# Sparse attention and a mixture of depths on one core: last queries' units in pairs, the gate row through DRAM, the mixture over 27 steps

## The chip, the cores and the metric

The kernel runs on one core of a Trainium2 chip. The metric is the time of one execution in microseconds (us). The core's engines are TensorE (PE, its weight loads PEld), VectorE (DVE), ScalarE (ACT), GpSimd (POOL) and SyncE (SP, which here only issues DMAs).

## The reference

Attention in which each query keeps the 32 largest scores of its row, then a layer in which each batch's 128 tokens with the largest gate go through a small network. B is 8 batches, H 8 heads, S 576 tokens, D 64; the bridged width is 512, the network's hidden width F 1024.

```python
scores = (1 / sqrt(D)) * q @ k.T                    # per batch and head
kth = np.partition(scores, -32, axis=-1)[..., -32:-31]
scores = np.where(scores >= kth, scores, -1e9)
attn = softmax(scores)                              # with + 1e-09 in the denominator
x = (attn @ v) -> (B, S, H * D)
# mixture: per batch b
s = x[b] @ w_gate
top = the 128 tokens with the largest s
ye = relu(x[b, top] @ w1) @ w2
out[b, top] = x[b, top] + sigmoid(s[top])[:, None] * ye     # other rows: x
```

## The kernel before

All data is float32. The 576 queries of a batch are four tiles of 128 (`t` 0 to 3, token 4p + t on partition p) and a last one of 64 (`t == J`). A unit is one query tile and one pair of heads; a unit of `t < J` holds two tiles of [128, 576] scores, one for each head. In a unit of last queries the two heads' 64 rows are stacked into one tile. A batch has 16 units of two tiles and 4 of one tile, 20 in all; eight batches make 160.

The main loop is a software pipeline written out by hand. Step `n` works on six units at once; every engine takes its instructions in the order in which the loop issues them:

- unit `n + 1`: `multiply` (PE, products of q and k into the PSUM tile `ps`) and `keep` (ACT, `sc`);
- unit `n`: `find_bound` (DVE: maxima of eighths `cand`, then three rounds of `best`), a bound below which no score can be among the 32;
- unit `n - 1`: `cut` and `part` (ACT, `sides`), then on POOL `y = sc * sides` and `fill`;
- unit `n - 2`: `find_kth` (DVE, `next8`), the 32nd score;
- unit `n - 3`: `mask` (`less`): the first tile on ACT, a second one on POOL;
- unit `n - 4`: `turn` and `turn_last` (PE: each 128-wide block of scores is turned and out-of-reach scores are pushed down by a second matmul with `less`; eight blocks into `ptr`, and the last 64 keys of both tiles as a ninth into a corner of `ps`), exponentials (ACT, `pT` and `last`), `values` (PE, into `av`) and `keep_values` (ACT, `xs`).

`ps` has one buffer, so the products of a step wait until ACT has read the turned last block. When a query tile's heads are done, two steps follow it: DVE inverts the sums (`sums`, `rden`), and POOL writes `x` (`normalise`) and DVE the gate product (`gates`, `prod`). After `t == J` SP stores `x` to `out`.

The mixture of batch `b - 1` is a generator that the loop advances by one piece in each step of batch `b` from `mix_at` on: the gate row is turned on PE and copied by ACT so that it stands on every partition (`gate_row`, two pieces); DVE counts for each token how many gates are larger (`junk`, `ranks`) and marks its place (`pick`), in three pieces; PE and DVE make the row numbers (`place_ps`, `row_i`); POOL gathers the rows (`xe`, an indirect DMA); PE turns them and DVE makes their gate (`xe_ps`, `g`); three pieces of the first layer (`h_ps`, 12, 12 and 8 matmuls), four of the second (`y_ps`, two each); ACT scales (`gy`), POOL adds the rows to `out` by an indirect DMA (the scatter). The next batch's q and k rows are fetched by SP and turned by PE at the steps of `load_at` (`rows`, `tr`). In the trace each float32 matmul of the program stands as two.

PSUM rooms named `misc` (one buffer) serve row transposes, gate transposes and all mixture products in turn.

Of the kernel before, what the change touches and what calls it, by code (L numbers as in the profile page):

```python
# [45 lines left out]
def kernel(  # L46
# [36 lines left out]
    modpool = ctx.enter_context(tc.tile_pool(name="mod", bufs=1))  # L83
    PS = bass.MemoryType.PSUM
# [37 lines left out]
    NS = B * NHP * (2 * J + 1)  # L122
# [20 lines left out]
    for i in range(2):  # L143
        vt = const.tile([P, H, J, DE], FP32, name=f"v{i}")
        nc.gpsimd.memset(vt, 1.0)
        vlast = const.tile([R, H, DE], FP32, name=f"vlast{i}")
        nc.gpsimd.memset(vlast, 1.0)
# [4 lines left out]
        vbufs.append((vt, vlast, vpair))  # L152
# [96 lines left out]
    def load_v(vb, vs):  # L249
        vt, vlast, vpair = vs  # L250
        v_rows = vb[:, JP:S, :].rearrange("h p d -> p h d")
        sp.dma_start(out=vlast[:, :, 0:D], in_=v_rows)
# [10 lines left out]
    def heads_of(t):  # L263

        return [[(0, 0), (1, R)]] if t == J else [[(0, 0)], [(1, 0)]]
# [4 lines left out]
    def multiply(t, hp, kT, qT, ps):  # L274
# [16 lines left out]
    def keep(n, ps):  # L291

        sc = scpool.tile([P, 2, S], FP32, name="sc")
        for i in range(n):
# [6 lines left out]
    def find_bound(n, sc):  # L301
# [7 lines left out]
        for i in range(n):  # L309
            for u in range(8):  # L310
                dve.max(cand[:, i, 8 * u : 8 * u + 8], sc[:, i, u * w : (u + 1) * w])
        for r in range(3):
            for i in range(n):
                dve.max(best[r][:, i, :], cand[:, i, :])
            if r < 2:
                for i in range(n):
# [5 lines left out]
    def cut(n, best, at):  # L322

        act.copy(
            out=seen[:, 0, at : at + n],
            in_=best.rearrange("p i e -> p (i e)").bitcast(BF16)[:, 15 : 16 * n : 16],
        )
# [16 lines left out]
    def fill(n, y, at):  # L344

        pool.tensor_tensor(
            y[:, 0:n, S : S + 8],
            steps[:, 0:n, :],
            seen[:, 2, at : at + n].unsqueeze(2).to_broadcast([P, n, 8]),
# [3 lines left out]
    def find_kth(n, y):  # L353

        next8 = stats.tile([P, 2, 8], FP32, name="next8")
        for i in range(n):
# [3 lines left out]
    def mask(n, sc, next8):  # L360

        less = wkpool.tile([P, 2, S], BF16, name="less")
        for i in range(n):
# [33 lines left out]
    def turn_last(n, z, ps, less=None):  # L397
# [4 lines left out]
        tr = ps[0 : n * R, 1, 1, 512 - P : 512]  # L402
        last = [
            a and a.rearrange("p i s -> p (i s)")[:, JP : JP + n * R] for a in (z, less)
# [4 lines left out]
    def values(t, hp, i, pT, last, av, vs):  # L409

        vt, vlast, vpair = vs
        n = R if t == J else P
        for hh, r in heads_of(t)[i]:
            o = av[0:n, hh * DE : (hh + 1) * DE]
            for c in range(J):
                pe.matmul(
                    o,
                    pT[:, i, c, r : r + n],
                    vt[:, 2 * hp + hh, c, :],
                    start=(c == 0 and i == 0),  # L420
                    stop=(c == J - 1 and t < J),
                    skip_group_check=(i == 1),
                )
            if t == J:
                pe.matmul(
                    o,
                    last[0:R, r : r + n],
                    vlast[:, 2 * hp + hh, :],
                    start=False,
                    stop=True,  # L430
                )
# [3 lines left out]
        if i == 1:  # L435
# [9 lines left out]
    def keep_values(t, hp, av, xs):  # L445
        n = R if t == J else P
        act.copy(
            out=xs[0:n, 2 * hp : 2 * hp + 2, :].rearrange("p h e -> p (h e)"),
            in_=av[0:n, 0 : 2 * DE],
        )  # L450
# [53 lines left out]
    def mixture(row0, gate, rank, exact=False):  # L504
# [7 lines left out]
        tr = ps_misc.tile([P, 512], FP32, name="tr", tag="misc")  # L512
        for t in range(J):
            pe.transpose(
                tr[:, t * P : (t + 1) * P],
                gate[:, t : t + 1].to_broadcast([P, P]),
                ident,
            )
        late.append(lambda tr=tr: act.copy(out=gate_row[:, 0:JP], in_=tr))

        yield
        tr = ps_misc.tile([P, 512], FP32, name="tr", tag="misc")
        pe.transpose(
            tr[:, 0:R], gate[0:R, J:NT].to_broadcast([R, P]), ident[0:R, 0:R]
        )
        late.append(lambda tr=tr: act.copy(out=gate_row[:, JP:S], in_=tr[:, 0:R]))
# [3 lines left out]
        for t in range(NT):  # L530
            if t % 2 == 0:
                yield
# [57 lines left out]
        yield  # L590
# [92 lines left out]
    units = [(b, t, hp) for b in range(B) for t in range(NT) for hp in range(NHP)]  # L683
    per_batch = NT * NHP


    load_at = (0, 1, 10, 11, 12, 13, 16, 17, 18)
# [8 lines left out]
    mix_at = 14  # L696
    first_tile, tiles = [], 0
    for b, t, hp in units:
        first_tile.append(tiles)
        tiles += len(heads_of(t))  # L700
# [268 lines left out]
```

## Time and profile before

| | us |
|---|---|
| median of 3 runs | 1003.89 (1003.25 to 1007.76) |
| profiled execution, own time | 1007.97 |
| its span (first to last instruction) | 1006.2 |
| PE busy | 948.5 (94%) |
| DVE busy | 866.1 (86%) |
| ACT busy | 804.9 (80%) |
| POOL busy | 709.5 (71%) |

The profiled execution lies 1.8 us over its span and 0.4% over the median. A busy share is a mean over the whole span; batches and single steps are read with windows. A step is taken from the start of one unit's last-block turn on PE to that of the next.

### The profile page before, as it was taken

To read this page: it belongs to the slowest core of one execution; us is meant where nothing else is said; L and a number is where in the kernel's file an instruction comes from. 1 tells how busy PE (TensorE), PEld (TensorE's weight loads), DVE (VectorE), ACT (ScalarE), POOL (GpSimd) and SP (SyncE) were. 2 spreads that over 40 slices of the span, in tenths; PEclk is the share of its full clock that TensorE was granted. 3 is DMA by queue.
4 is the path that set the end of the run, shared out by engine and by line. 5 is a ranking of instruction groups with operands and counts; after the bars stand their busy time and mean duration, and the time that the engine had idled before them with its cause. 6 is when DMAs were issued, how large, how long until landed. Compare 5 with 4: busy or idle time off the path is not lost.

```text
span 1006.2 us, 24785 instructions
## 1 busy us (share of the span) xinstructions
PE 948.5 (94%) x7922; PEld 760.4 (76%) x7922; DVE 866.1 (86%) x4966; ACT 804.9 (80%) x1945; POOL 709.5 (71%) x818
## 2 busy tenths in 40 slices
PE   5799999999999999999999999999999999999856
PEld 3588777786878878887878878788778878777734
DVE  4899899999989998899988998899988999899130
ACT  3799899998779887898889897898889987797300
POOL 3688768984778767895778857886768957797110
PEclk9999999999999999999999999999999999999778
DMA  5942012112203112111212122111122010000110
GB/s 107 260 95 56 2 53 59 39 37 75 60 1 65 33 65 58 33 38 43 76 32 54 32 75 59 21 44 44 53 59 38 17 54 7 1 12 2 53 26 14
DMA packets 123833, 49.12 MB, mean 49 GB/s; under 512 B 118960, under 2 KB 118960, under 8 KB 122672
## 3 DMA queue, kind: packets, MB, share of 16 engines
q1 hardware_dynamic: 120320, 42.88, 16.8%
q0 software_dynamic: 1792, 4.20, 2.3%
q8 instruction: 65, 1.06, 0.4%
q10 hardware_dynamic: 1584, 0.39, 0.2%
q14 instruction: 72, 0.59, 0.2%
HBM read 35.91 MB, written 11.53 MB: 47 GB/s over the span
## 4 chain that ended last, share of the span: by engine, by line
PE 59%; ACT 15%; DVE 14%; POOL 8%; issue 2%; DMA 1%; SPq 0%; ACTq 0%; POOLq 0%
PE av L42 19%; PE ps L42 13%; PE ptr L42 13%; PE h_ps L42 6%; DVE cand L42 6%; PE y_ps L42 5%; ACT sides L42 5%; POOL y L42 4%; ACT sc L42 4%; DVE next L42 3%; POOL less L42 3%; PE tr L42 2%; ACT pT L42 2%; DVE best L42 2%; ACT less L42 1%
## 5 line engine op out<-in xcount | busy, mean ns | idle before, releaser
L42 POOL TENSOR_TENSOR y<-sc,sides 128x576 f32<-128x576 f32 x288 | 369.9, 1314 | 176.1 <-ACT sides L42 170.4
L42 DVE MAX8 cand<-sc 128x8 f32<-128x72 f32 x2304 | 323.8, 217 | 36.5 <-ACT sc L42 36.4
L42 PEld LDWEIGHTS av<-v,pT 128*128 128x128 f32 (+1 forms) x2560 | 274.8, 182 | 68.1 <-issue 26.1
L42 PE MATMUL av<-v,pT 128*128 128x65 f32 (+1 forms) x2560 | 301.6, 269 | 2.8 <-ACT pT L42 2.8
L42 DVE MAX8 next<-y 128x8 f32<-128x584 f32 x288 | 206.6, 754 | 35.7 <-POOL y L42 35.5
L42 POOL TENSOR_SCALAR less<-sc,next 128x576 bf16<-128x576 f32 x128 | 224.1, 1751 | 4.8 <-DVE next L42 4.3
L42 ACT ACTIVATE sides<-sc,seen 128x576 bf16<-128x576 f32 x288 | 221.3, 769 | 7.4
L42 PE MATMUL ptr<-ident,sc 128*128 128x128 f32 x1152 | 217.8, 281 | 0.0
L42 PE MATMUL ps<-kT,qT 64*128 64x288 f32 (+1 forms) x1280 | 203.2, 437 | 10.7 <-ACT last L42 5.8
L42 ACT ACTIVATE pT<-ptr 128x512 f32<-128x512 f32 x288 | 168.9, 596 | 50.7 <-PE ptr L42 42.7
L42 PE MATMUL ptr<-out_of_reach,less 128*128 128x128 bf16 x1152 | 206.4, 220 | 0.0
L42 ACT COPY sc<-ps 128x576 f32<-128x576 f32 x288 | 171.3, 646 | 10.6 <-PE ps L42 10.6
L42 PEld LDWEIGHTS ptr<-ident,sc 128*128 128x128 f32 x1152 | 162.7, 141 | 15.8
L42 DVE MAX8 best<-cand 128x8 f32<-128x64 f32 x864 | 154.5, 216 | 3.3
L42 PEld LDWEIGHTS <-less 128*128 128x128 bf16 (+1 forms) x1312 | 137.3, 105 | 23.2 <-POOL less L42 11.2
L42 PEld LDWEIGHTS ps<-kT,qT 64*128 64x128 f32 (+1 forms) x1280 | 106.3, 180 | 59.1 <-issue 20.8
L42 ACT ACTIVATE less<-sc,next 128x576 bf16<-128x576 f32 x160 | 124.4, 777 | 6.8 <-DVE next L42 6.5
L42 DVE MATCH_REPLACE8 cand<-best,cand 128x64 f32<-128x64 f32 x576 | 116.5, 209 | 0.0
L42 ACT ACTIVATE last<-ps 128x128 f32<-128x128 f32 (+1 forms) x160 | 43.8, 274 | 57.7 <-PE ps L42 56.9
L42 PE MATMUL h_ps<-xeT,w 128*128 128x128 f32 x512 | 66.5, 289 | 3.1 <-ACT hT L42 1.7
L42 PEld LDWEIGHTS h_ps<-xeT,w 128*128 128x128 f32 x512 | 63.1, 203 | 5.1 <-ACT hT L42 2.4
L42 POOL TENSOR_TENSOR x<-xs,rden 128x512 f32<-128x512 f32 (+1 forms) x40 | 41.7, 1042 | 33.6 <-DVE rden L42 33.6
(83 smaller groups left out, 919.2 us busy)
## 6 DMA issues: line engine op xcount, KB each, us to landing
rows<-in_k_dram SPq DMA_DIRECT2D x64, 128.0 KB, 2.9
v<-in_v_dram SPq DMA_DIRECT2D x64, 128.0 KB, 3.0
out_dram<-x SPq DMA_DIRECT2D x8, 1024.0 KB, 4.8
rows<-in_q_dram SPq DMA_DIRECT2D x62, 128.0 KB, 2.7
w<-in_moe_w_dram SPq DMA_DIRECT2D x2, 2048.0 KB, 13.4
last<-in_k_dram SPq DMA_DIRECT2D x8, 128.0 KB, 3.7
vlast<-in_v_dram SPq DMA_DIRECT2D x8, 128.0 KB, 3.0
vpair<-in_v_dram SPq DMA_DIRECT2D x16, 64.0 KB, 2.8
```

What stands on the lines that cost most here:

```text
L42: return lambda *a, **kw: self._tc.keep_in_program_order(fn(*a, **kw))
```

## The change

1. A unit of last queries now holds four heads in two tiles: in each tile two heads are stacked, heads 4g and 4g + 2 in the first, 4g + 1 and 4g + 3 in the second. Their products use four quarters of PE's array (rows by the head's half of the partitions, columns by its place in the stack), their values two column halves in turn. The last keys' values of such units come from the zero-padded `vpair` as for all others; `vlast` and its DMA are gone. Each batch has 18 units of two tiles, so every step is of one size, and the helper functions lose the argument for the number of tiles.
2. The gate row goes through DRAM: two DMAs write the gates in token order, a third reads them back onto all partitions. The last batch's mixture (`over`) still turns it on PE.
3. The mixture has 17 pieces, each rank of its own, at the steps of a table `mix_at` that reaches over two batches, so that two mixtures overlap; the first piece runs in step 5 of the next batch. After the last unit the loop advances the last but one mixture by two pieces a step. `load_at` is spread differently as well.

Here the step of a batch is n modulo 18; units of last queries have their values in steps 2 and 3 and their products in steps 15 and 16.

```diff
-        vlast = const.tile([R, H, DE], FP32, name=f"vlast{i}")
...
-        sp.dma_start(out=vlast[:, :, 0:D], in_=v_rows)
...
-    def heads_of(t):
-        return [[(0, 0), (1, R)]] if t == J else [[(0, 0)], [(1, 0)]]
+    def groups(t):
+        return NHP // 2 if t == J else NHP
+    def heads_of(t, g):
+        if t == J:
+            return [[(4 * g + i, 0), (4 * g + 2 + i, R)] for i in range(2)]
+        return [[(2 * g + i, 0)] for i in range(2)]
...
-    def multiply(t, hp, kT, qT, ps):
+    def multiply(t, g, kT, qT, ps):
         n = R if t == J else P
         for u in range(2):
-            for i, heads in enumerate(heads_of(t)):
+            for i, heads in enumerate(heads_of(t, g)):
                 at = u * HALF + (0 if i else R)
-                for hh, r in heads:
-                    d = slice(hh * D, (hh + 1) * D)
+                d = slice(i * D, (i + 1) * D)
+                for h, r in heads:
                     pe.matmul(
                         ps[r : r + n, i, u, 0:HALF],
-                        qT[d, hp, t * P : t * P + n],
-                        kT[d, hp, at : at + HALF],
+                        qT[d, h // 2, t * P : t * P + n],
+                        kT[d, h // 2, at : at + HALF],
                     )
...
+        for i, heads in enumerate(heads_of(t, g)):
             for c in range(J):
+                for h, r in heads:
+                    pe.matmul(
+                        av[r : r + n, i * DE : (i + 1) * DE],
+                        pT[:, i, c, r : r + n],
+                        vt[:, h, c, :],
...
+        for h, r in heads_of(t, g)[0]:
             pe.matmul(
-                av[:, 0 : 2 * DE],
-                last,
-                vpair[:, hp, :, :].rearrange("p h e -> p (h e)"),
+                av[r : r + n, 0 : 2 * DE],
+                last[:, r : r + n],
+                vpair[:, h // 2, :, :].rearrange("p h e -> p (h e)"),
...
+            row_dram = drampool.tile([1, S], FP32, name="row_dram")
+            sp.dma_start(
+                out=row_dram[0, 0:JP].rearrange("(p j) -> p j", j=J), in_=gate[:, 0:J]
+            )
+            sp.dma_start(
+                out=row_dram[0, JP:S].rearrange("(p j) -> p j", j=1),
+                in_=gate[0:R, J:NT],
+            )
+            sp.dma_start(out=gate_row, in_=row_dram.to_broadcast([P, S]))
...
         for t in range(NT):
-            if t % 2 == 0:
-                yield
+            yield
...
-    load_at = (0, 1, 10, 11, 12, 13, 16, 17, 18)
+    load_at = (2, 4, 6, 8, 14, 15, 16, 17, 18)
...
-    mix_at = 14
+    mix_at = (5, 7, 9, 10, 11, 12, 13, 14, 19, 21, 23, 25, 27, 28, 29, 30, 31)
...
+        for b in mix_steps.get(n, ()):
+            next(mixtures[b], None)
+        if n >= N:
+            for _ in range(2):
+                next(mixtures[B - 2], None)
+                flush()
```

PE, values of a one-tile unit of last queries in the last step of a batch's four (the names are the PSUM and SBUF tiles; `x4` counts the program's matmuls), before:

```order
L42 MATMUL ps<-kT,qT 128x288 x4
L42 MATMUL av<-v_124,pT 64x65 x4
L42 MATMUL av<-vlast_126,last 64x65
L42 MATMUL av<-v_124,pT 64x65 x4
L42 MATMUL av<-vlast_126,last 64x65
L42 MATMUL h_ps<-xeT,w_141 128x128 x12
```

and the second of a batch's two merged units after the change:

```order
L42 MATMUL ps<-kT,qT 128x288 x4
L42 MATMUL av<-v_132,pT 64x65 x16
L42 MATMUL av<-vpair_134,last 64x130 x2
L42 MATMUL h_ps<-xeT,w_139 128x128 x12
L42 MATMUL ps<-ident,sc 128x128
```

Four such groups of ten matmuls a batch have become two of eighteen, and the separate `vlast` matmuls are gone.

SP's DMAs from the store of a batch's `x` to the next batch's rows and values, before:

```order
L42 DMA out_dram<-x 128x2048
L42 DMA out_dram<-x 64x512
L42 DMA vlast_126<-in_v_dram 64x8x64
L42 DMA vpair_128<-in_v_dram 64x4x64 x2
L42 DMA v_124<-in_v_dram 128x4x64 x8
L42 DMA rows<-in_k_dram 128x4x64 x2
```

after:

```order
L42 DMA out_dram<-x 128x2048
L42 DMA out_dram<-x 64x512
L42 DMA row_dram<-gate 128x4
L42 DMA row_dram<-gate 64x1
L42 DMA gate_row<-row_dram 128x576
L42 DMA rows<-in_k_dram 128x4x64 x2
L42 DMA vpair_128<-in_v_dram 64x4x64 x2
```

Three DMAs now stand between the store of `x` and the next batch's rows and values.

## Rows read from the trace of the kernel before

**Rows 1.** The page, part 1: busy us, share, instructions.

```profile
PE 948.5 (94%) x7922; PEld 760.4 (76%) x7922; DVE 866.1 (86%) x4966; ACT 804.9 (80%) x1945; POOL 709.5 (71%) x818
```

**Rows 2.** Windows over batches 0, 1, 4 and 6 (columns in the first line).

```profile
core 0: us, PE busy (x) PEld busy (x) DVE busy (x) ACT busy (x) POOL busy (x), PEclk, DMA share, GB/s
37.32:143.89 106.57, 103.05 (x908) 83.78 (x909) 99.32 (x594) 97.58 (x240) 83.82 (x98) 1.00 0.32 82
...
143.89:255.69 111.80, 106.54 (x937) 86.77 (x936) 110.66 (x617) 99.78 (x244) 88.65 (x102) 0.98 0.19 47
...
488.06:604.25 116.19, 115.04 (x992) 93.27 (x991) 107.02 (x619) 100.26 (x243) 87.89 (x100) 1.00 0.20 48
...
720.45:835.04 114.59, 113.91 (x981) 92.26 (x979) 105.45 (x616) 98.54 (x237) 87.11 (x99) 1.00 0.15 37
```

**Rows 3.** Windows over single steps: row transposes, gate transposes, one-tile unit, plain step.

```profile
534.21:539.56 5.35, 5.35 (x51) 4.62 (x50) 3.73 (x24) 5.32 (x14) 4.17 (x5) 1.00 0.59 98
550.25:556.01 5.76, 5.52 (x50) 4.57 (x49) 5.76 (x36) 5.46 (x14) 5.08 (x7) 1.00 0.40 91
...
587.07:591.70 4.63, 4.63 (x44) 3.49 (x43) 4.60 (x34) 3.64 (x10) 2.56 (x4) 1.00 0.01 4
...
875.84:880.75 4.91, 4.91 (x45) 4.17 (x44) 3.04 (x16) 4.02 (x9) 4.76 (x6) 1.00 0.00 2
```

**Rows 4.** Timeline of PE, plain step from 875.84: start, us, instructions.

```profile
877.47 1.24 PE L42 MATMUL ps<-kT,qT 64*128 64x288 f32 x8
878.64 2.00 PE L42 MATMUL av<-v,pT 128*128 128x65 f32 x16
...
880.75 0.27 PE L42 MATMUL ps<-ident,sc 128*128 128x128 f32 x1
```

**Rows 5.** Timeline of PE, products and values of a one-tile step.

```profile
477.56 1.24 PE L42 MATMUL ps<-kT,qT 64*128 64x288 f32 x8 [0.77 <-ACT last L42]
478.73 0.68 PE L42 MATMUL av<-v,pT 128*64 128x65 f32 x8
479.34 0.33 PE L42 MATMUL av<-vlast,last 64*64 64x65 f32 x2
...
480.46 0.66 PE L42 MATMUL xe_ps<-ident,xe 128*128 128x128 f32 x4
```

**Rows 6.** Timeline of PE, products of a one-tile unit and what follows.

```profile
568.15 1.19 PE L42 MATMUL ps<-kT,qT 64*64 64x288 f32 x8
569.26 2.00 PE L42 MATMUL av<-v,pT 128*128 128x65 f32 x16
```

**Rows 7.** Timeline of PE and DVE behind the last values.

```profile
957.43 7.13 PE L42 MATMUL y_ps<-w,hT 128*128 128x512 f32 x16
...
960.06 0.07 DVE L42 DVE_READ_ACCUMULATOR2_ANT gate<- 64x1 f32 x1
...
965.35 0.65 PE L42 MATMUL tr<-ident,gate 128*128 128x128 f32 x4 [0.78 <-ACT gy L42]
```

**Rows 8.** DMA issues: KB each, median us from issue to landing.

```profile
rows<-in_k_dram SPq DMA_DIRECT2D x64, 128.0 KB, 2.9
...
out_dram<-x SPq DMA_DIRECT2D x8, 128.0 KB, 2.3
...
out_dram<-gy,row_i POOLq DMA_INDIRECT x8, 4.9
```

**Rows 9.** Chain of waits in batch 1: bounds and 32nd scores on DVE.

```profile
159.07 2.16 DVE cand L42 x16
...
162.79 1.33 DVE next L42 x2
...
212.56 1.09 DVE cand L42 x8
...
215.07 1.34 DVE next L42 x2
```

**Rows 10.** The page, part 5: busy us, mean ns of one.

```profile
L42 PEld LDWEIGHTS av<-v,pT 128*128 128x128 f32 (+1 forms) x2560 | 274.8, 182 | 68.1 <-issue 26.1
```

**Rows 11.** Groups of DVE in batch 4: busy us, mean ns of one.

```profile
L42 DVE CUSTOM_DVE_ANT_0 prod<-xe,wg 128x512 f32<-128x512 f32 x1 | 1.5, 1519 | 0.0
```

More of the change, by code (lines that the diff above doesn't have):

```diff
@@ L308, in find_bound @@
         best = [stats.tile([P, 2, 8], FP32, name=f"best{r}") for r in range(3)]
-        for i in range(n):
+        for i in range(2):
             for u in range(8):
@@ L502, in break_ties, with mixture @@
         )
-    def mixture(row0, gate, rank, exact=False):
+    def mixture(row0, gate, rank, exact=False, over=False):
         gate_row = modpool.tile([P, S], FP32, name="gate_row")
[L512 to L517, printed above, removed]
-            )
-        late.append(lambda tr=tr: act.copy(out=gate_row[:, 0:JP], in_=tr))
-        yield
[L522 to L526, printed above, removed]
+        if exact or over:
+            for t0, t1, at in ((0, J, 0), (J, NT, JP)):
+                tr = ps_misc.tile([P, 512], FP32, name="tr", tag="misc")
+                n = R if t0 else P
+                for t in range(t0, t1):
+                    pe.transpose(
+                        tr[:, (t - t0) * P : (t - t0) * P + n],
+                        gate[0:n, t : t + 1].to_broadcast([n, P]),
+                        ident[0:n, 0:n],
+                    )
+                w = (t1 - t0) * n
+                act.copy(out=gate_row[:, at : at + w], in_=tr[:, 0:w])
+        else:
+            row_dram = drampool.tile([1, S], FP32, name="row_dram")
+            sp.dma_start(
+                out=row_dram[0, 0:JP].rearrange("(p j) -> p j", j=J), in_=gate[:, 0:J]
+            )
+            sp.dma_start(
+                out=row_dram[0, JP:S].rearrange("(p j) -> p j", j=1),
+                in_=gate[0:R, J:NT],
+            )
+            sp.dma_start(out=gate_row, in_=row_dram.to_broadcast([P, S]))
         pick = modpool.tile([P, NT, CAP], BF16, name="pick")
         for t in range(NT):
-            if t % 2 == 0:
-                yield
+            yield
             n = R if t == J else P
@@ L694 @@
     v_at = 6
-    mix_at = 14
[L697 to L700, printed above, removed]
+    mix_at = (5, 7, 9, 10, 11, 12, 13, 14, 19, 21, 23, 25, 27, 28, 29, 30, 31)
+    mix_steps = {}
+    for b in range(B - 1):
+        for i in mix_at:
+            n = (b + 1) * per_batch + i
+            if n >= N:
+                break
+            mix_steps.setdefault(n, []).append(b)
+    mixtures = {}
     qkv = {0: room_for_qkv(0)}
@@ L709, with is_unit @@
     scs, bests, ys, next8s, masks = {}, {}, {}, {}, {}
-    def tiles_of(n):
-        return len(heads_of(units[n][1])) if 0 <= n < len(units) else 0
-    for n in range(-1, len(units) + 6):
+    def is_unit(n):
+        return 0 <= n < N
+    for n in range(-1, N + 6):
         if 0 <= n + 1 < NHP:
@@ L804 @@
                 store(out[b], of_batch[b][0])
-        b, i = divmod(n, per_batch)
-        if 0 < b < B and i == mix_at:
-            mixing = mixture(float((b - 1) * S), of_batch[b - 1][1], ranks[:, b - 1, :])
-        next(mixing, None)
-        if n >= len(units):
-            flush()
-            next(mixing, None)
+                mixtures[b] = mixture(
+                    float(b * S), of_batch[b][1], ranks[:, b, :], over=(b == B - 1)
+                )
+        for b in mix_steps.get(n, ()):
+            next(mixtures[b], None)
+        if n >= N:
+            for _ in range(2):
+                next(mixtures[B - 2], None)
+                flush()
         if n in load_steps:
@@ L822 @@
     flush()
-    for _ in mixing:
-        flush()
-    for _ in mixture(float((B - 1) * S), of_batch[B - 1][1], ranks[:, B - 1, :]):
-        flush()
+    for b in (B - 2, B - 1):
+        for _ in mixtures[b]:
+            flush()
     sure = stats.tile([P, 1], FP32, name="sure")
@@ L860, with general_weights @@
     )
-    def general_weights(n, sc):
+    def general_weights(sc):
         p = wkpool.tile([P, 2, S], FP32, name="p", tag="y")
-        for i in range(n):
+        for i in range(2):
             cur, tops = sc[:, i, :], []
@@ L911, in general @@
                 last = ptpool.tile([P, P], FP32, name="last")
-                for i in range(w):
+                for i in range(2):
                     nc.scalar.copy(
@@ L916, in general @@
                     )
-                nc.scalar.copy(out=last[0 : w * R, :], in_=turn_last(w, p, ps))
-                for i in range(w):
-                    values(t, hp, i, pT, last, av, vs)
-                keep_values(t, hp, av, xs)
+                nc.scalar.copy(out=last, in_=turn_last(p, ps))
+                values(t, g, pT, last, av, vs)
+                keep_values(t, g, av, xs)
             rows = R if t == J else P
```

163 lines of the change are left out of this document (73 added, 90 removed).

## The prediction

> **What bounds the kernel now.** I read the page's busy shares first, then windows over whole batches, then windows over single steps, then TensorE's (PE's) timeline inside a step, and the chain of waits where PE is not the bound. PE is busy for 94% of the span, VectorE (DVE) for 86% [rows 1]. By batches [rows 2] the reader is to see two regimes. In the steady ones (488.06 to 604.25; three more read the same) PE is busy for 115.04 of 116.19 us, DVE for 107.02. In the batch from 143.89, where half of a mixture of experts is missing on PE, DVE is busy for 110.66 of 111.80. So PE bounds batches 2 to 6, and DVE stands 8 us behind it.
>
> By steps [rows 3]: a plain step takes 4.91 us, all of it PE's, with DVE at 3.04. A step with four row transposes takes 5.35 (so they cost 0.44), one with the four gate transposes has 5.52 of PE, and a step that turns one tile of last queries takes 4.63 with four row transposes, 4.19 without. Inside the plain step [rows 4]: the nine turned blocks end at 877.47 (1.63 us), the scores' products at 878.64 (1.17), the values at 880.75 (2.11). Inside a one-tile step [rows 5] the products start 0.77 late, since ScalarE (ACT) must first read the last block out of the same PSUM tile; then 1.17 for products and 1.73 for values. That leaves 4.19 - 1.17 - 1.73 = 1.29 for turning.
>
> **The change, part by part.** All sums are for one steady batch, against 116.19.
>
> *Merged units.* A batch now has four one-tile value steps at 4.19, four steps whose products are those of last queries, and twelve plain ones. Such products run on two quarters of the array, in 1.11 [rows 6], so these steps take 4.91 - 1.17 + 1.11 = 4.85. Sum: 12 x 4.91 + 4 x 4.85 + 4 x 4.19 = 95.1. The rest of PE's 115.04, 19.9, is row transposes, mixture and gate transposes.
>
> After the change there are 14 plain steps (68.7), two with merged products of time M and two with merged values of time V. They take 3.74 + M and 1.63 + 1.17 + V = 2.80 + V.
>
> M: twice as many matmuls as the 1.11 holds, now on four quarters. If all four run side by side M stays 1.11; if only two do, it is 2.2. The row nearest is that same one: eight matmuls of 288 columns in 1.11 us. Sixteen y matmuls of 512 columns take 7.13 [rows 7], 0.87 ns a column, so eight of 288 one after another would need 2.0: quarters that share neither rows nor columns do run in pairs now. What no row shows is two quarters that share rows. I take 1.11. By the Trainium skill (TensorEngine Tiling (Array Packing), Key Properties) tiles work independently and load and multiply in parallel, which would give this same 1.11 and the low end for V; no row here has two such tiles.
>
> V: 32 matmuls of 64 weight columns that move 65 columns, and four that move 130, in alternating column halves. One after another: eight now take 0.61 (478.73 to 479.34) [rows 5], 0.076 each, so 2.43, plus four times 130 columns at 0.87 ns, 0.45: 2.9. Side by side in twos: 1.45. Loading weights may bind either way, and the mode no longer changes for the last block, which it did four times in 1.73; I take 2.0, just below the middle.
>
> So PE's steps come to 68.7 + 2 x 4.85 + 2 x 4.8 = 88.0; ends 86.9 (1.11 and 1.45) and 92.0 (2.2 and 2.9). The gain is 7.1 of PE, between 3.1 and 8.2.
>
> *Gate row through DRAM.* It removes five transposes: four cost 5.52 - 4.91 = 0.61 [rows 3, 4], so 0.8 with the fifth, and one read of each from PSUM by ACT. It adds three DMAs on SP, behind the store of x: two small writes that wait for the last gate product on DVE, and a read that waits for both. The nearest rows land in 2.3 and 2.9 us [rows 8], so 5 to 8 us with the issues (the read moves 295 KB). The first rank comes two steps later, over 10 us. Hidden at no cost; with that cover gone DVE would stall for the excess. Behind the waiting SP stand the next batch's rows and values. Rows are fetched three or more steps ahead of their transposes, so nothing waits for them.
>
> *Spread mixture.* PE's mixture work is only moved, and PE was continuous in the steps that held it, so the move itself saves little there. It puts ranks of one batch (DVE) beside y products of the one before (PE, four steps), which keeps DVE's extra work in PE's longest steps. The scatter is now one step ahead of the next gather, which must wait for its landing, 4.9 us [rows 8]; a step of 5.2 covers it on GpSimd (POOL).
>
> *DVE and POOL.* Bounds for two tiles cost DVE 3.72 (159.07 to 162.79), for a lone tile 2.51 (212.56 to 215.07) [rows 9]. Four lone tiles less save 4 x (2.51 - 1.86) = 2.6: DVE's busy time goes to 104.4. A plain step's own work on DVE is 5.05 (159.07 to 162.79 and 1.33 more). POOL gets two masks more and ACT two fewer; POOL has 28 us to spare a batch [rows 2].
>
> *Sum.* PE: 115.04 - 7.1 - 0.8 = 107.1, ends 106.0 and 111.1. Of the 1.15 that PE idles now, 0.77 stands ahead of a one-tile step's products and goes, as a full set of blocks lies there. But DVE, at 104.4, is now only 2.7 behind, and in step 1 of a batch it needs 5.05 + 1.5 for the gathered rows' gate [rows 11] + 0.2 where PE needs 4.91 + 0.5. It may trail by a step without stopping PE, so I add 1.4: 108.5 a batch, 7.7 less.
>
> - Batches 2 to 5: 4 x 7.7 = 31; batch 6, now 114.59, 6.
> - Batch 0 (106.57 now, 103.05 of PE, 99.32 of DVE): PE falls by 7, DVE stays near 97, and the first step's waits remain: 100.5, 6 less.
> - Batch 1: on DVE already, so the 2.6, two steps' hand-overs, and a little of the rank work that now lies later: 107, 5 less.
> - Batch 7 and the end: 8 for its units. Then the end: last values were done at 957.43, but 7.13 of y stood between them and the last batch's gate transposes at 965.35, although the gate itself was ready at 960.1 [rows 7]. With two steps of mixture 6 in each draining step, about half of y is left there: 4 less. 12 together.
>
> 31 + 6 + 6 + 5 + 12 = 60: the span goes from 1006.2 to 946, the profiled execution from 1007.97 to 948. The three runs have a median of 1003.89, 0.4% under the profiled one, so **944 us**.
>
> **Rivals.**
> 1. *Quarters in the same rows take turns* (M 2.2, V 2.9): the merging then does not do what it is for, and only saved blocks and mode changes remain. PE 111.1, batch 112; 4 x 4.2 + 2.6 + 4 + 5 + 9 = 37: 966. For it: no row shows such an overlap. Against it: loads and products of values, all in the same rows, already overlap, since 18 take 2.11, 0.117 each [rows 4], while one load alone lasts 0.18 [rows 10]. By the Trainium skill (TensorE: Matmul & The Clock Gate, The mechanism) a weight load overlaps matmuls in flight only where the row group differs, and here it never does: that is this rival's time. The rows of this kernel disagree with it in its strict form.
> 2. *DVE becomes the bound.* If no step lends time to the next, each takes the longer of PE and DVE. By the new order DVE exceeds PE by 1.3 in step 1, by 0.8 in step 13 (a gate product and the row numbers), by 0.5 in step 17 and by 0.5 in four others together: 3.1 over 107.1. Batch 110.2: 4 x 6.0 + 4.4 + 6 + 5 + 10 = 49: about 954. For it: batch 1 now. Against it: PE had no gap in the steps in which DVE trailed.
> 3. *Slower: each change of quarter drains the array.* A one-tile step's 20 value matmuls would stream in 20 x 65 x 0.87 ns = 1.1 but take 1.73: up to 0.15 for each of four changes of mode. If a change of half cost 0.1 as well, 2 x (35 + 15) changes make 10 us a batch on top of rival 1's 112: 122, and 1003.9 + 6 x 5.8 - 4 = 1035. It is slower from 0.04 a change on. Against it: plain products alternate between the array's row halves and still take 1.17 for eight.
> 4. *The gate row comes late*: over 10 us for three DMAs would stall DVE. It would have to be over 18 to make a batch slower; rows of 2.3 and 2.9 speak against it.
>
> **How the numbers follow.** My forecast 0.62 (930 to 957); rival 2 0.13; rival 1 0.15; rival 3 0.03; better than the low ends, under 930, 0.05; something else 0.02. The range must leave out no more than 0.2: it runs from 928, where both merges are at their low ends and nothing idles (10 a batch, 76 in all), to 970, which takes in rivals 1 and 2. A change under 0.5%, 5 us, is about what a measurement of this kernel cannot tell from none. Only rival 3 is slower, 0.03; within 0.5% needs a mishap between rivals 1 and 3, 0.02; faster 0.95.
>
> **What would show it.** In a steady batch of the new profile: 18 steps in 107 to 110 us; a merged value step of 4.6 to 5.0 of PE without its extras, its 32 matmuls in 1.3 to 1.9; 16 merged products in 1.1; no gate transposes but in the last batch; PE busy over 97% and DVE over 94%; the gate row's read landed before its first rank, with no DVE idle there. Wrong: values at 0.07 or more a matmul (rival 1), an idle PE behind masks that wait for DVE (rival 2), the last batch's gate transposes as late behind the last values as now (the end).

## The result and the profile after

The changed kernel takes 964.95 us (median of four runs, 962.42 to 971.46) where the kernel before, timed beside it, takes 1005.01: a ratio of 0.961, 95% interval 0.955 to 0.967. The profiled execution took 966.9 us with a span of 964.8, 41.4 less than the 1006.2 of before; the prediction had 60.

The page of the changed kernel, part 1 and the chain by engine: busy us, share of the span, instructions; then the engines' shares of the chain that ended last.

```profile
PE 885.8 (92%) x7791; PEld 718.1 (74%) x7791; DVE 853.4 (88%) x4966; ACT 780.6 (81%) x1883; POOL 736.1 (76%) x800
...
DVE 40%; PE 37%; POOL 8%; ACT 7%; DMA 4%; issue 3%; SPq 0%; POOLq 0%; ACTq 0%
```

PE has lost 62.7 us of work against [rows 1], but the span only 41.4, and its share has fallen from 94% to 92%: PE waits more than before. Its part of the chain that ended last has fallen from 59% to 37%, and DVE's has grown from 14% to 40%. The same windows as in [rows 2], batches 0, 1, 4, 6 and the last one with the end:

```profile
core 0: us, PE busy (x) PEld busy (x) DVE busy (x) ACT busy (x) POOL busy (x), PEclk, DMA share, GB/s
35.87:138.63 102.76, 98.90 (x893) 81.75 (x893) 95.74 (x589) 94.12 (x231) 86.82 (x96) 0.93 0.31 74
138.63:246.88 108.25, 100.62 (x918) 82.72 (x918) 106.58 (x629) 96.36 (x237) 91.32 (x99) 0.95 0.21 50
...
468.60:579.91 111.31, 106.90 (x976) 87.73 (x974) 107.07 (x619) 97.41 (x236) 91.92 (x98) 1.00 0.22 52
...
691.33:802.44 111.11, 106.26 (x967) 87.14 (x966) 105.57 (x619) 96.85 (x234) 92.08 (x98) 1.00 0.20 49
802.44:964.80 162.36, 131.70 (x1047) 103.08 (x1045) 101.81 (x543) 87.39 (x210) 88.41 (x93) 0.92 0.10 21
```

The steady batch is the one to read. PE's busy time is what the prediction said (106.90 for 107.1), but the batch takes 111.31 for 108.5: PE idles for 4.4 us where 1.4 had been allowed, and DVE is busy for 107.07, as before, where 104.4 had been expected. The other steady batches take 110.8 to 111.4.

Where PE idles: windows over single steps of that batch, columns as above. The first three are steps 15, 16 and 17, the other two the steps with the merged values (2 and 3 of the next batch's count).

```profile
536.05:542.27 6.22, 5.47 (x58) 4.36 (x56) 4.34 (x28) 4.49 (x11) 4.52 (x5) 1.00 0.37 86
542.27:548.47 6.20, 5.70 (x57) 4.42 (x57) 5.15 (x34) 5.34 (x14) 6.20 (x9) 1.00 0.39 89
548.47:555.40 6.93, 5.58 (x48) 4.66 (x49) 6.90 (x44) 6.28 (x15) 6.69 (x7) 1.00 0.17 38
566.53:572.17 5.64, 4.82 (x73) 3.77 (x72) 5.61 (x32) 4.80 (x14) 4.99 (x5) 1.00 0.01 1
572.17:579.91 7.74, 7.01 (x87) 6.03 (x87) 7.71 (x51) 7.64 (x22) 6.21 (x7) 1.00 0.01 2
```

These five hold 4.15 of the 4.4 us. In the first of them DVE, too, is busy for only 4.34 of 6.22. From 545.8 to 570.2 the chain of waits then lies on DVE, with POOL and ACT on either side of it, and returns to PE only at 574.65: the idle time in the two value steps is what this delay leaves. The waits of DVE in the same batch (in all, times, longest):

```profile
DVE next L42 <- POOL y L42: 2.9, 2, 1.9
DVE junk L42 <- DMA gate_row<-row_dram: 0.8, 1, 0.8
```

DVE waits for `y` of GpSimd (POOL). POOL's own timeline around it (start, us, instruction, idle time before it):

```profile
528.00 1.72 POOL L42 TENSOR_SCALAR less<-sc,next 128x576 bf16<-128x576 f32 x1
...
530.01 1.65 POOL L653 DMA_INDIRECT out_dram<-gy,row_i  x1
533.32 1.99 POOL L42 TENSOR_SCALAR less<-sc,next 128x576 bf16<-128x576 f32 x1 [1.66 <-DVE next L42]
...
535.76 1.05 POOL L590 DMA_INDIRECT xe<-out_dram,row_i  x1 [0.32 <-issue]
536.85 2.52 POOL L42 TENSOR_TENSOR y<-sc,sides 128x576 f32<-128x576 f32 x2
...
541.21 1.73 POOL L42 TENSOR_SCALAR less<-sc,next 128x576 bf16<-128x576 f32 x1 [1.67 <-PE av L42]
...
543.04 2.52 POOL L42 TENSOR_TENSOR y<-sc,sides 128x576 f32<-128x576 f32 x2
...
545.70 2.51 POOL L42 TENSOR_TENSOR y<-sc,sides 128x576 f32<-128x576 f32 x2
```

In the code, masks (`less`) and `y` alternate. Here two masks stand between 528 and 535, and two `y` between 543 and 548. ACT's signs (`sides`) for the `y` that starts at 536.85:

```profile
530.22 0.78 ACT L42 ACTIVATE sides<-sc,seen 128x576 bf16<-128x576 f32 x1
530.90 0.19 ACT L42 ACTIVATION_READ_ACCUMULATOR sides<-sc,seen 128x1 f32 x1
```

Half of the signs are there at 531.1. That `y` could have run from 531.7 at the latest, when the scatter was out, in POOL's own idle time; it came 5.2 us later, behind a mask that had to wait for DVE and behind the gather. The reason is in the code. All other POOL instructions of the main loop go through `InOrder`, which ties each to the one issued before it on its engine; scatter and gather go through `nc.gpsimd` and are tied to nothing, so the scheduler may hoist them. The order in the trace tells that what is issued behind them is tied only to them: the next step's mask passes the `y` of this step. So the statement on the kernel before, that every engine takes its instructions in the order of the loop, does not hold for these two. Before the change, a gather followed ten steps behind a scatter (532.20 and 583.56 in the batch of [rows 2]); now they stand in neighbouring steps, and two such shifts follow each other.

What the merging itself gave: pieces of the chain of waits (start, us, what): sixteen merged products, and the 36 value matmuls of a merged step.

```profile
537.75 1.13 PE ps L42 x16
...
575.89 1.31 PE av L42 x36
```

Sixteen products take what eight took in [rows 6], and the values less than the low end of 1.45.

The gate row, on SP's queue, in the steady batch:

```profile
478.74 4.74 SPq L42 DMA_DIRECT2D row_dram<-gate  x2
490.48 0.32 SPq L42 DMA_DIRECT2D gate_row<-row_dram  x1
```

The last gate was ready on DVE at 482.94 and the second write (0.2 KB) went out at 482.98; the read could be issued only at 490.48, and the first rank began at 494.19. That is 11.2 us, not 5 to 8. The 0.8 us that DVE waited for it fell into steps in which PE did not wait. In the whole span DVE waits for it 2.9 us, in five batches.

The end: where the chain leaves the last values, and then DVE, POOL and PE on their timelines:

```profile
915.71 3.65 PE y_ps L42 x8
```

```profile
916.53 0.19 DVE L42 RECIPROCAL rden<-sums 64x8 f32<-64x8 f32 x1
923.12 0.68 DVE L42 CUSTOM_DVE_ANT_0 prod<-x,wg 64x512 f32<-64x512 f32 x1 [6.40 <-POOL x L42]
...
920.35 1.65 POOL L653 DMA_INDIRECT out_dram<-gy,row_i  x1 [17.90 <-ACT gy L42]
921.48 1.60 POOL L42 TENSOR_TENSOR x<-xs,rden 64x512 f32<-64x512 f32 x1
...
920.12 0.65 PE L42 MATMUL tr<-ident,gate 128*128 128x128 f32 x4 [0.78 <-ACT gy L42]
923.96 0.24 PE L42 MATMUL tr<-ident,gate 64*128 64x64 f32 x1 [3.19 <-DVE gate L42]
```

POOL, idle for 17.9 us, had `x` of the last queries queued behind the scatter of mixture 6, which waited for PE's `y_ps`. The denominators were ready at 916.7, `x` began at 921.5, and the last gate was ready at 923.8. Half of `y_ps` has gone from between, as the prediction said, and four gate transposes stand 4.4 us behind the last values for 7.9 in [rows 7]; but the fifth stands 8.3 behind, and the ranks need all. From the last values to the end it takes 49.1 us, where it was 48.8.

### The profile page after: what moved, and what is told of

It reads as the page before. It is cut to its first block, busy times and chain, and to the rows that moved or that the text cites. A ratio compares the mean times of both kernels' runs of the same rounds, so it can differ in the third digit from the quotient of the medians.

```text
span 964.8 us, 24451 instructions
## 1 busy us (share of the span) xinstructions
PE 885.8 (92%) x7791; PEld 718.1 (74%) x7791; DVE 853.4 (88%) x4966; ACT 780.6 (81%) x1883; POOL 736.1 (76%) x800
## 4 chain that ended last, share of the span: by engine, by line
DVE 40%; PE 37%; POOL 8%; ACT 7%; DMA 4%; issue 3%; SPq 0%; POOLq 0%; ACTq 0%
DVE cand L42 19%; PE av L42 11%; DVE next L42 10%; PE ps L42 8%; PE ptr L42 8%; PE h_ps L42 5%; DVE best L42 5%; POOL y L42 4%; PE y_ps L42 4%; POOL less L42 2%; DVE prod L42 2%; ACT sides L42 2%; DMA row_dram<-gate 2%; ACT sc L42 2%; DVE junk L42 2%
## 5 line engine op out<-in xcount | busy, mean ns | idle before, releaser
L42 PEld LDWEIGHTS av<-v,pT 128*128 128x128 f32 (+1 forms) x2560 | 256.7, 182 | 56.9 <-issue 23.5
L42 PE MATMUL av<-v,pT 128*128 128x65 f32 (+1 forms) x2560 | 276.9, 269 | 0.1
L42 POOL TENSOR_SCALAR less<-sc,next 128x576 bf16<-128x576 f32 x144 | 249.8, 1735 | 22.3 <-DVE next L42 16.3
L42 PE MATMUL ps<-kT,qT 64*128 64x288 f32 (+1 forms) x1280 | 186.1, 442 | 8.6 <-ACT last L42 4.5
L42 ACT COPY sc<-ps 128x576 f32<-128x576 f32 x288 | 170.0, 649 | 11.3 <-PE ps L42 11.2
L42 PEld LDWEIGHTS <-less 128*128 128x128 bf16 x1296 | 135.1, 105 | 34.1 <-POOL less L42 27.0
L42 DVE MAX8 best<-cand 128x8 f32<-128x64 f32 x864 | 148.9, 214 | 0.0
L42 PEld LDWEIGHTS ps<-kT,qT 64*128 64x128 f32 (+1 forms) x1280 | 100.2, 182 | 51.3 <-issue 18.4
L42 ACT ACTIVATE less<-sc,next 128x576 bf16<-128x576 f32 x144 | 112.1, 778 | 17.1 <-DVE next L42 17.1
L42 ACT ACTIVATE last<-ps 128x128 f32<-128x128 f32 x144 | 39.7, 275 | 41.3 <-PE ps L42 40.7
L42 PE MATMUL av<-vpair,last 128*128 128x130 f32 (+1 forms) x320 | 63.0, 298 | 0.0
```

Of the source, the lines that this page charges most:

```text
L42: return lambda *a, **kw: self._tc.keep_in_program_order(fn(*a, **kw))
```

## The experiments

Theory A: the loss is the order on POOL. Rivals: B, DVE has become the bound by its own work and by waits for the SBUF port that it shares with POOL; C, the gate row. All twelve start from the changed kernel (964.95, ratio 0.961); ratios are to the kernel before, timed beside each. No run takes the gate row away: C is judged by DVE's waits for it alone.

**1. Scatter and gather in code order.**

```diff
-        nc.gpsimd.indirect_dma_start(
+        pool.indirect_dma_start(          # both
```

> The scatter and the gather of a mixture take the place in GpSimd's queue that they have in the code, behind the products y of their step; nothing else changes. Theory A (the changed kernel loses its time on GpSimd: the two transfers, which the scheduler is free to hoist, stand in neighbouring steps, and each lets a mask and a transfer pass the y of the step before; DVE then waits 1.9 and 1.05 us for y in each steady batch and trails PE for the next six steps): DVE's waits for y go, PE's idle time falls from 4.4 us a batch to 1.5 to 2.5, a steady batch from 111.1 to 108.5 to 109.5, and with batch 1 the time falls by 12 to 16, to 949 to 953. Theory B (DVE has simply become the bound, by its work and by waits for GpSimd's port): under 0.5 us a batch, 961 to 965. Theory C (the gate row through DRAM is what costs): no change, 965.

Measured: 953.65 us (952.39 to 957.73), ratio 0.948 (0.945 to 0.951). The batch:

```profile
461.92:571.21 109.29, 106.56 (x975) 87.67 (x974) 107.56 (x619) 96.92 (x236) 91.25 (x98) 1.00 0.24 53
```

POOL's queue now has `y` between scatter and gather:

```profile
527.86 1.64 POOL L42 DMA_INDIRECT out_dram<-gy,row_i  x1 [0.17 <-issue]
529.02 2.27 POOL L42 TENSOR_SCALAR less<-sc,next 128x576 bf16<-128x576 f32 x1
...
530.85 3.04 POOL L42 TENSOR_TENSOR y<-sc,sides 128x576 f32<-128x576 f32 x2
...
534.23 1.07 POOL L42 DMA_INDIRECT xe<-out_dram,row_i  x1 [0.17 <-DVE cand L42]
```

DVE's waits for `y` are gone from the view, PE's idle time is 2.7 and the batch 109.3: the upper end of what A said for the batch, while idle time and total lie just above A's. Batches 2 to 6 are each 1.4 to 2.1 us shorter than in the changed kernel, 9.0 together, and this comes from the place of two instructions in POOL's queue. B and C had nothing near it. Not all of the 11.3 us between the two medians can be put down to it: batch 0, which holds neither transfer, is 4.3 us shorter as well (98.47 for 102.76), with a granted clock of 0.97 for 0.93, and batch 1 is 1.0 longer.

```profile
35.54:134.01 98.47, 94.66 (x892) 78.63 (x892) 95.48 (x589) 93.65 (x231) 86.67 (x96) 0.97 0.33 80
```

**2. The same, and the gather two steps later.**

```diff
-    mix_at = (5, 7, 9, 10, 11, 12, 13, 14, 19, ...
+    mix_at = (5, 7, 9, 10, 11, 12, 13, 16, 19, ...
```

> As the run before, and the gather two steps later (16 for 14), so that it cannot stand on GpSimd for the scatter's landing. Theory A: as the run before or up to 1 us a batch better, 943 to 952; if the wait for the landing were the whole of the loss and the order nothing, the run before would stay at 961 to 965 and this one alone come to 950. Theories B and C: 961 to 965.

Measured: 971.85 us (968.10 to 972.67), ratio 0.965 (0.962 to 0.967): worse than either theory, at 111.1 a batch. (Batch 1 and the last one with the end take 2.9 and 5.1 us more than in run 1, at granted clocks of 0.92 and 0.88 for 0.95 and 0.91.) So the landing of the scatter was not the loss. What happened instead, on POOL and DVE near the gather's new place:

```profile
553.90 1.73 POOL L42 TENSOR_SCALAR less<-sc,next 128x576 bf16<-128x576 f32 x1
...
555.73 2.51 POOL L42 TENSOR_TENSOR y<-sc,sides 128x576 f32<-128x576 f32 x2
558.21 0.21 POOL L42 TENSOR_TENSOR y<-steps,seen 128x16 f32<-128x16 f32 x1
558.40 2.15 POOL L42 TENSOR_SCALAR less<-sc,next 128x576 bf16<-128x576 f32 x1
...
555.41 3.56 DVE L42 CUSTOM_DVE_ANT_0 prod<-x,wg 128x512 f32<-128x512 f32 x1
```

DVE's gate product, 0.68 us in the rows of the end above, lasts 3.56: it is through half a microsecond after POOL's run of back-to-back instructions has ended (558.42), and POOL's next mask then takes 2.15 for 1.73. In the batch the five products take 8.3 us where run 1 has 6.5, and DVE is busy for 109.09 where it has 107.56. The gather in step 16 stands ahead of `x`, so that POOL's mask and `y` come to lie over DVE's product; that is read from the rows, no run tests it. It is B's mechanism, set off by POOL's order. The kernel before has it too: in its batch 1 a product takes 4.42 (from 154.64) beside POOL's instructions without a pause. By the Trainium skill (GPSIMD Engine Reference, Specifications) POOL shares its SBUF interfaces with DVE instructions that have two inputs in SBUF or run in a two-port mode; the product, with two inputs in SBUF, agrees with it in these rows.

**3 and 4. The small addition to the denominators on ACT,** once in the changed kernel, once on top of run 1.

```diff
-        dve.tensor_scalar_add(out=den[0:n, :], in0=xs[0:n, :, D], scalar1=1e-9)
+        act.activation(den[0:n, :], xs[0:n, :, D], AF.Copy, bias=1e-9)   # behind keep_values
```

The reason, DVE's groups in the steady batch of the changed kernel (busy us, mean ns of one), where before the five additions took 1.1 and the five products 4.0:

```profile
L42 DVE CUSTOM_DVE_ANT_0 prod<-x,wg 128x512 f32<-128x512 f32 (+1 forms) x5 | 5.2, 1045 | 0.0
L42 DVE TENSOR_SCALAR sums<-xs 128x8 f32<-128x8 f32 (+1 forms) x5 | 3.7, 733 | 0.0
```

> The small addition to the denominators (sums, 128x8, five a batch) is done by ACT in place of DVE; in the changed kernel it takes DVE 0.73 us each in a steady batch, 0.15 where no y of GpSimd is under way. GpSimd's order is that of the changed kernel. Theory A: the waits for y stay, only the trailing after them is caught up sooner: 0.5 to 1.5 us a batch, 955 to 962. Theory B: DVE is the bound, and its 3.7 us a batch come back nearly whole: 2.5 to 3 a batch, 944 to 950. Theory C: 965.

Measured: 961.18 (958.12 to 962.30), ratio 0.954 (0.952 to 0.957); batches of 110.7 to 111.4. DVE's waits for `y` stay (4.0 us in a steady batch), as A has it.

> The scatter and gather in code order (as in the first run, 953.65) and the small addition to the denominators on ACT. What remains idle on PE in that run is 2.3 us a steady batch of 109.3. Theory B' (DVE's instructions with two inputs in SBUF, and the small addition, stand until GpSimd's back-to-back instructions end; that delay is the rest): 1 to 2 us a batch less, 941 to 947. Theory A' (the rest is GpSimd's own crowd of x, scatter and gather in three steps that follow each other, so that a mask comes late): 0 to 0.5 a batch, 950 to 954.

Measured: 950.70 (948.85 to 952.43), ratio 0.944 (0.941 to 0.947); batches of 109.05 at full clock. DVE's busy time in a batch falls by 2.4 (107.07 to 104.68) and by 3.2 (107.56 to 104.3), and a steady batch gets only 0.2 to 0.3 shorter. So B falls as the main cause. (In run 3's profiled execution 2.7 us lie in batch 0, at a granted clock of 0.96 for 0.93.)

**5. Scatter, x and gather two steps apart,** in code order; ranks beside y.

```diff
-    mix_at = (5, 7, 9, 10, 11, 12, 13, 14, 19, 21, 23, 25, 27, 28, 29, 30, 31)
+    mix_at = (5, 7, 8, 9, 10, 11, 12, 15, 19, 20, 21, 22, 25, 26, 27, 28, 29)
-    load_at = (2, 4, 6, 8, 14, 15, 16, 17, 18)
+    load_at = (5, 6, 11, 13, 14, 15, 16, 17, 18)
```

> In code order again, and other steps for the mixture and the loads: scatter in step 11, x of a tile in 13, gather in 15, where they are now in 13, 13 and 14; ranks in 7 to 11, y in 7 to 10. Theory A': the mask that comes 1.7 us late in step 15 is in time, a batch takes 107.8 to 108.5, 945 to 949. Theory B': the port delays move but stay, 109 to 110 a batch, 952 to 957.

Measured: 952.50 (949.14 to 953.80), ratio 0.944 (0.941 to 0.947); batches 2 to 6 of 108.9 to 110.2. By the total it is not to be told from run 1, and it fits B' (952 to 957), not A', while run 4 fits A' (0 to 0.5 us a batch): what is left after run 1 has no one cause that these runs show. Two changes offset each other: batches 1 to 3 are 0.5 to 1.4 longer than there, and the last batch with the end takes 158.4 us for 162.7. The two batches at full granted clock take 108.95, 0.35 less than in run 1; the longer ones of batches 2 to 6 all have 0.98.

**6. At the end, x ahead of the scatter,** in code order.

```diff
-        if n >= N:
+        if N <= n < N + 4:
             for _ in range(2):
                 next(mixtures[B - 2], None)
```

> In code order again, and behind the last units the x of the last queries stands ahead of the scatter of the last mixture but one on GpSimd, where now it waits behind it for y on PE. If GpSimd's order is what kept the last batch's gate late (the record's four us for the end): the gate is ready at 4 to 5 us less behind the last values, and the end is 3 to 4 us shorter: 949.5 to 951. If the y products on PE kept it late: the four gate transposes stay behind them and 0 to 1 us comes back: 952.5 to 954.

Measured: 951.38 (949.52 to 956.93), ratio 0.946 (0.941 to 0.950). `x` on POOL, and the gate transposes on PE:

```profile
904.57 1.04 POOL L42 TENSOR_TENSOR x<-xs,rden 64x512 f32<-64x512 f32 x1 [14.42 <-DVE rden L42]
...
907.82 0.65 PE L42 MATMUL tr<-ident,gate 128*128 128x128 f32 x4 [0.78 <-ACT gy L42]
909.15 0.27 PE L42 MATMUL tr<-ident,gate 64*128 64x64 f32 x1 [0.68 <-ACT gate_row L42]
```

The fifth transpose starts 1.3 us behind the four, for 3.8; the last batch with the end takes 159.5 for 162.7. This is the first case, though the total lies just above its 951: POOL's order had been the hindrance. The four still wait for ACT's reading of `y_ps`, and the fifth now only for ACT's copy of the gate row.

**7 and 8. The mixture's products in one run of steps,** as they stood before the change; first with the transfers free, then in code order.

```diff
-    mix_at = (5, 7, 9, 10, 11, 12, 13, 14, 19, 21, 23, 25, 27, 28, 29, 30, 31)
+    mix_at = (5, 10, 11, 12, 13, 14, 15, 16, 18, 19, 20, 21, 22, 23, 24, 25, 26)
-    load_at = (2, 4, 6, 8, 14, 15, 16, 17, 18)
+    load_at = (8, 9, 10, 11, 12, 13, 14, 16, 17)     # and v_at = 8 for 6
```

> The changed kernel with one part undone: the mixture's products stand in steps that follow each other (ranks 10 to 14, rows 16, products in steps 0 to 7 of the next batch, scatter in 8), the loads in 8 to 17; merged units and the gate row by DMA stay, and the two transfers stay free to be hoisted. The record's step (PE's work is only moved; ranks away from y make DVE the bound in five steps of 5.35): 110 to 112 a batch, 960 to 970. If spreading was what gained: 114 or more a batch, over 980. Theory A: scatter and gather are eight steps apart, so DVE's two waits for y no longer follow each other, and half of the 2.9 us goes: 108 to 110 a batch, 950 to 960.

Measured: 985.21 (982.81 to 985.65), ratio 0.978 (0.976 to 0.980); batches of 113.3 to 114.2.

> The mixture's products in one run, as in the run of 985.21, with scatter and gather in code order. If what cost there was the hoisted gather (it stood 2.9 us on GpSimd for its row numbers, ahead of y): 109 to 110.5 a batch for 113.3 to 114.2, 958 to 966. If what cost was that the ranks no longer lie beside y, so that DVE is the bound in five steps: 112 to 114 a batch, 975 to 985.

Measured: 974.10 (970.50 to 982.80), ratio 0.966 (0.964 to 0.969); a batch of the profiled execution, which is the longest of the four (982.80), and the waits of PE in it:

```profile
473.58:586.06 112.48, 108.26 (x975) 88.49 (x974) 105.40 (x619) 97.48 (x236) 91.15 (x98) 0.98 0.25 51
```

```profile
PE ps L42 <- POOL less L42: 4.1, 3, 2.4
```

In code order, the spread schedule is worth 112.5 - 109.3 = 3.2 us a batch in these executions, 1.5 of it idle time of PE and 1.7 its busy time, at a granted clock of 0.98 for 1.00; by the medians of runs 8 and 1 it is 20 us in all. With the transfers free it is 2 to 3 a batch, at 0.97 to 0.99. Of the three cases for run 7 only the one by which spreading was what gained (over 980) holds, and its batch was set slightly too high. Run 8's batch lies in its second case, but that DVE is the bound there is not shown: PE waits for masks of POOL, and DVE itself waits 6.6 us in the batch. The loads had to move as well (18 steps hold nine loads and nine uses of the one PSUM bank they share), so this is the price of the schedule as a whole, not of ranks alone.

**9 and 10. Merged matmuls ordered by halves of the array,** in groups of four, then one half after the other. The cut shows the values; the products are reordered as well.

```diff
-            for c in range(J):
-                for h, r in heads:
+            for h, r in heads:           # run 10: outside the loop over i too
+                for c in range(J):
```

> The same matmuls of the merged steps in another order: all of one half of the array's columns, then all of the other, where now each matmul is followed by one of the other half. If matmuls in two column halves of the same rows run side by side only where they stand next to each other: 36 value matmuls go from 1.31 us to 2.4 to 2.9, 16 merged products from 1.13 to 2.0 to 2.2, 4.4 us of PE a batch, of which 2 to 4 are seen (PE waits in two of the four steps): 980 to 995. If the halves do not overlap and the gain came from fewer changes of mode and fewer blocks alone: the values stay within 0.15 of 1.31, 963 to 968.

> Matmuls of the merged steps ordered further apart than in the run of 969.0: all sixteen values of one column half, then all of the other; products two by two on each quarter. If two column halves run side by side only as far as PE looks ahead: 36 values take 2.2 to 2.9 us (1.31 in turn, 1.70 in fours), 2 to 3 us a batch, 972 to 985. If the order is worth the 0.4 of the run in fours and no more: values 1.7 to 1.9, 968 to 972.

Measured: 969.00 (968.31 to 973.44), ratio 0.963 (0.961 to 0.964), and 972.62 (two runs), ratio 0.966 (0.964 to 0.969). The 36 values, in fours (two records are missing) and then by halves (PE's timeline):

```profile
578.95 1.70 PE av L42 x34
```

```profile
574.36 1.73 PE L42 MATMUL av<-v,pT 128*64 128x65 f32 x29
575.87 0.33 PE L42 MATMUL av<-vpair,last 128*64 128x130 f32 x1
575.92 0.28 PE L42 MATMUL av<-v,pT 128*64 128x65 f32 x2
...
576.41 0.82 PE L42 MATMUL h_ps<-xeT,w 128*128 128x128 f32 x5
```

1.31 in turn, 1.70 in fours, 2.05 by halves (574.36 to 576.41), all at full granted clock. The sixteen products hardly change: 1.13 in run 9 and 1.15 in run 10, where 2.0 to 2.2 had been expected of run 9. By their totals runs 9 and 10 are not to be told from the changed kernel with certainty; the rows tell them apart. Two column halves do run side by side, and for the values the more so the closer their matmuls stand. I had expected 2.4 to 2.9 in fours; neither run's two theories had a case for what came.

**11 and 12. What helped, together:** code order, addition on ACT, x first at the end; then with the steps of run 5 as well.

> The three edits that helped, together, with the steps of the change: scatter and gather in code order, the addition to the denominators on ACT, x of the last queries ahead of the scatter at the end. If the gains add (code order 11, the addition 2 to 3, the end 2 to 3, out of 965): 947 to 950. If the end's and the addition's gains are one and the same (both shorten the wait for the last x): 950 to 952.

> As the run before, with the scatter, x and gather two steps apart (11, 13, 15) and ranks and y moved with them. That move alone gave 1 us of 953.65, so by the sum 946 to 949. If the order of the steps is worth nothing once DVE is relieved: as the run before, within 2 us.

Measured: 949.61 (945.26 to 953.40), ratio 0.942 (0.940 to 0.945), and **943.14** (940.26 to 947.89), ratio 0.937 (0.935 to 0.940). The first lies in the range for gains that add; the second is below its 946 to 949. A batch of run 12, with a granted clock of 0.98; three others, at full clock, take 108.5:

```profile
456.60:566.48 109.88, 108.07 (x976) 88.74 (x974) 106.69 (x633) 97.96 (x240) 90.88 (x99) 0.98 0.25 52
```

The interval of run 12's ratio lies wholly below the changed kernel's: run 12 beats both kernels. What it has over run 11 lies in batch 1 (105.7 us for 109.0, at a granted clock of 1.00 for 0.94) and in the last batch with the end (155.7 for 160.6), hardly in the steady batches (108.5 to 109.9 for 109.0).

## Why the prediction was right, and where it was not

The time lay in the range and on the right side; the likeliest value was 21 us too low, and the time lies outside the 930 to 957 of the forecast's own case. The range held it because it was drawn to take in rivals 1 and 2. Of the signs that were named, the length of a batch, PE busy over 97% (96% in the steady batch) and the gate row without a wait of DVE did not come. By its steps, in the profiled executions:

- *Merged units.* Right, and better than taken: M 1.13 for 1.11, V 1.31 for 2.0, below the low end. Rival 1 falls (its V was 2.9), though its total of 966 is the nearest of all to the 964.95: that is chance. Its premise that the row group never differs holds for the values only; the merged products change the array's row half after every two. Rival 3 falls as well: a change of quarter costs nothing that shows, since matmuls that alternate are the fastest of runs 9 and 10 and of the changed kernel. PE's 106.90 agrees with the 107.1 partly by chance: 1.4 less for two V, and 0.7 us more in four steps (16, 17, 0 and 3), in which the turned blocks wait in part for late masks and take PE 1.75 to 1.86 for the 1.63 of the others.
- *DVE and POOL: 107.02 - 2.6 = 104.4.* This step failed. The additions and gate products take 3.2 us a batch more than before, held beside POOL's instructions (3.7 + 5.2 + 0.9 with the gathered rows' product, for 1.1 + 4.0 + 1.5 [rows 11]), which uses up the 2.6. In the batch as it ran this cost little: runs 3 and 4 take the additions off DVE and give back 0.2 to 0.3. "POOL has 28 us to spare" is true of the sum and says nothing of the moment: POOL holds DVE up while it is itself busy.
- *Spread mixture: "the scatter is now one step ahead of the next gather ... a step of 5.2 covers it on POOL".* This is the step that missed most. The landing was covered: the scatter had landed at 534.98, and the gather began at 535.76. What was not seen is that both transfers may be hoisted, and what they do to the order of masks and `y`: 2.0 of the 2.8 us that the steady batch shown missed (111.3 for 108.5), as run 1 shows; 1.4 to 2.1 in the others. I read the order of PE and SP, not POOL's.
- *"The move itself saves little."* Also wrong, the other way: it is worth 2 to 3 us (runs 7 and 8). Without it much of what the merging frees on PE is idle time: 4.2 us a batch in run 8. By this the parts don't add: one takes work from PE, the other puts DVE's extra work where PE still has some. That is a reading; no run spreads the mixture without merged units.
- *Gate row: 5 to 8 us, hidden.* 11.2, and hidden: the cover was the "over 10" of the text with 0.8 us missing, off PE's path in the steady batch. In batches 1, 3 and 7 the chain that ended last does run through it, by way of DVE.
- *The sum.* Batches 2 to 5: 20.3 for 31; batch 6, 3.5 for 6: the idle time above. Batch 0, 3.8 for 6, and batch 1, 3.5 for 5: in the first two steps of batch 0 the granted clock was 0.50 and 0.75 in the changed kernel's profile (1.00 before), and for parts of batch 1 it was below full, so these two terms are not settled; in the twelve runs batch 0 took 97.8 to 102.0, at granted clocks of 0.98 to 0.93. Another 1.5 us were saved ahead of batch 0, for nothing in the sum.
- *The end: 12 with the units of batch 7.* 8.8, and 9.1 of it ahead of the end of the last values (8 were taken): the four us of the end did not come. It was named as what would show the step wrong ("gate transposes as late behind the last values as now"); the cause was POOL's order, and run 6 gave back 3.2 of them.
- *Rival 2* (each step takes the longer of two engines, 110.2 a batch, 954) foresaw part of the loss, but not its mechanism: in step 15 DVE idles more than PE. Run 1 takes 1.7 of the 4.4 us of idle time away with DVE's busy time no smaller (107.56 for 107.07).

What stays open: the 2.7 us a batch that PE still idles in run 1. 1.7 of them stand in step 15 (7.19 us with 5.48 of PE), ahead of a mask that POOL has behind `y` and the gather. Relieving DVE or spacing POOL's extras moved it little (2.5 and 2.2); with both, a batch of run 12 has 1.8. DVE's wait for the gate row, 1.2 us in run 1's batch, was not taken away in any run.

## What to carry to other kernels

Where one call is outside the order that all others keep, it doesn't only move itself: what is issued behind it passes what stands ahead of it; look at the queue of every engine on which a moved step issues anything, and read an engine's spare time by the moment, not by the sum. A short instruction can last several times its own length while another engine runs without a pause; what that costs has to be tried: run 2's batch grew by 1.8 us with it, while taking the held additions away gave 0.2 to 0.3 (runs 3 and 4). Matmuls in different column halves of the array are worth placing next to each other in the program: the same 36 took 1.31 us in turn and 2.05 one half after the other.

## What the runs showed of the hardware

- Two column halves of PE in the same rows overlap, weight loads of 0.14 us too: 36 matmuls in 1.31 us, 0.036 each, where eight in one half took 0.61, 0.076 each [rows 5]. In run 10 a matmul of one half (`vpair`, 575.87) starts ahead of three of the other half that the program has before it.
- An addition of 128x8 on DVE takes 0.15 us, and up to 1.22 in the changed kernel and 2.48 in run 5; a gate product 0.68, and up to 3.56 in run 2 and 4.42 in the kernel before, beside a run of POOL's instructions in both. DVE's reciprocal of the same size stays at 0.20 throughout. Why the addition, with one tensor as input, is held as well, no run shows.
- A write of 64 pieces of 4 bytes, 0.2 KB, took 6.5 to 8.0 us to land (the four of seven whose landing the trace has, median 7.1); of four writes of 128 pieces of 16 bytes three took 2.2 to 3.2, and one 8.5.
